# Attention operands made without copies, and one tile for the last queries of two heads, in a planned three-stage kernel

## The chip, the core and the metric

The kernel runs on one core of a Trainium2 chip. The metric is the device time of one execution in microseconds. The engines are named as in the profile: PE (TensorE, the matmuls; PEld its weight loads), DVE (VectorE), ACT (ScalarE), POOL (GpSimd) and SP (SyncE, which issues nearly all DMA transfers).

## What is computed

```
# _attn_ref: q, k, v are (4, 8, 576, 64); blocks of 64 positions, causal by block
scores = where(block_i >= block_j, q @ k.T / 8, -1e9)
attn   = exp(scores - max); attn /= sum + 1e-9;  x = attn @ v      # -> (2304, 512)
# _moe_ref: one expert layer for all tokens, d_ff = 1024
h = x @ w_in; solu = h * softmax(h); ln = (solu - mean) / sqrt(var + 1e-6) * g_ln
x = ln @ w_out
# _moe2_ref: cosine routing to the best of 8 experts, then that expert only
expert = argmax(xn @ en.T / tau);  out[token] = gate * (relu(x @ w1[expert]) @ w2[expert])
```

## The kernel before

Three stages follow each other: attention, a first expert layer over 18 tiles of 128 tokens, and a second one that works through tiles of gathered tokens, expert by expert. All matmuls work with numbers split in a high and a low part, so that one product is two or three matmuls.

**Attention** works on items. Items 0 to 3 ("low") each hold queries 0 to 255 of two heads of the first batch, so that the first tiles of tokens are complete early; then one item per head follows, without those queries for the first eight heads. `attn_load` brings q and k of an item into a buffer R (q in partitions 0 to 63, k in 64 to 127). `attn_prep` makes four operands H, L, S2, M2 from it, of which each matmul contracts 128 partitions: `it.ops = ((L, H), (S2, M2))`. A head's high and low parts have to lie in both halves of the partitions. For items 0 and 1 a second load with the halves exchanged (`qkl`, buffer RX) gives that; for the others H and L are made for 128 partitions at once, and four copies by DMA within SBUF put the halves in their places, two of them one after the other:

```
for o, on, x, xn in ((sb, Sa, hb[0:64], Ha), (mb, Ma, lb[64:128], Lb), (lb[64:128], Lb, sb[0:64], Sa),
                     (hb[0:64], Ha, hb[64:128], Hb)):
    op("SP", .45, lambda o=o, x=x: nc.sync.dma_start(o, x), r=["pa", xn], w=[on], size=W // 4)
```

There are three sets of operands, used in turn by items. `attn_score` then works through steps s0 to s4, tiles of 128 queries against 128, 256, 384, 512 and 576 keys; s4 has only 64 queries, 512 to 575. Per tile: two products on PE, a maximum (DVE), an exponential with its sum (ACT); per group of tiles (`it.norm`) a small addition to the sums (POOL), a reciprocal (DVE) and a scale of each tile (POOL or ACT, `either`). `attn_trans` (t0 to t4) transposes the probabilities on PE and evicts them into TH (ACT) and, as the rest, TL (DVE). `attn_av` (a0, a1) multiplies with V; the result goes to DRAM tensors `xT`, from which `b_load` brings tiles of tokens.

**The first expert layer** needs w_in and w_out converted from 64-bit floats by integer operations (`conv_ops`: three on DVE, then a cast on ACT and a subtract on POOL per piece) into the tile `win`; `b_up`, `b_down`, `b_route` and `b_choose` are its four parts per tile of tokens.

**The order** of these two stages is made by a planner (`order`): each operation has an engine, a duration and what it reads and writes; a list scheduler starts, on the engine that is free, the ready operation of the highest priority. The priority comes from a table of due times, `DUE`, by kind of work (A loads and operands, S scores, T transposes, V products with V, C weights, U, D, R the expert layer) and item, and from the transfers' time `land`. `either` operations go to the engine that is free first. What the planner puts in order stands so in each engine's queue, and an engine works through its queue in that order. The second expert layer is written out by hand (`c_all`).

## Time and profile before

| | before |
|---|---|
| median of 3 runs | 804.76 us (804.27 to 806.49) |
| profiled execution | 808.63 us, span 806.9 us |
| PE, DVE, ACT, POOL busy | 716.0, 472.4, 440.3, 313.4 us |
| mean granted clock of PE | 0.958 of full speed |
| moved by DMA | 101.02 MB, mean 125 GB/s |

PE's busy time counts from a matmul's start to its modelled end, and neighbours overlap in the pipeline; a matmul of 512 columns in a dense row starts 0.23 us behind the one ahead and is shown with 0.39 us. So a busy PE may still have gaps between its starts. Busy shares are means over stages with different limits; the rows below are therefore taken by stretches of the span.

### The profile page before, as it was taken

The numbers are of one execution on the slowest core, as the hardware profiler recorded it, in microseconds if no ns is written. First come the engines' busy times: TensorE is split into PE (matmuls) and PEld (weight loads), VectorE is DVE, ScalarE is ACT, GpSimd is POOL, SyncE is SP. The second block draws the span as 40 slices with busy tenths as digits, with TensorE's granted clock in tenths as the row PEclk, the third lists the DMA queues.
The fourth block names the chain that finished last, engine by engine and source line by source line (L and its number), as shares of the span: only waits on it lengthen the run. The fifth ranks groups of instructions, "written<-read, shape, count | busy, mean of one in ns | idle before, by whom it ended". The sixth has DMA issues, their size and how long they took to land. (4 is left out here: it accounts for less than half of the span.)

```text
span 806.9 us, 12838 instructions
## 1 busy us (share of the span) xinstructions
PE 716.0 (89%) x3832; PEld 575.0 (71%) x3832; DVE 472.4 (59%) x1055; ACT 440.3 (55%) x1019; POOL 313.4 (39%) x493
## 2 busy tenths in 40 slices
PE   1579887999989999989999999778999989989994
PEld 1467756877767788778887777567788867867883
DVE  5788879789948746868754766342222166266221
ACT  5688678888857656869553644211212255255211
POOL 4457456745727533665544544221111111111120
PEclk9989978999999999989999999889999999989998
DMA  8997655336371530363012600158111158167110
GB/s 228 240 255 221 184 165 154 100 103 176 101 191 58 153 91 25 102 154 79 28 53 64 222 27 28 40 192 312 34 46 50 40 180 296 42 207 265 40 42 23
DMA packets 59890, 101.02 MB, mean 125 GB/s; under 512 B 14288, under 2 KB 26224, under 8 KB 59792
## 3 DMA queue, kind: packets, MB, share of 16 engines
q1 hardware_dynamic: 55856, 89.44, 37.8%
q0 software_dynamic: 3936, 10.51, 3.7%
q8 instruction: 32, 0.52, 0.3%
q14 instruction: 66, 0.54, 0.3%
HBM read 65.42 MB, written 15.11 MB: 100 GB/s over the span
## 5 line engine op out<-in xcount | busy, mean ns | idle before, releaser
L555 PE MATMUL banks<-wexp,workr 128*128 128x512 f32 x320 | 135.8, 424 | 3.6 <-ACTq L1056 2.9
L556 PE MATMUL banks<-wexp,workr 128*128 128x512 f32 x320 | 129.9, 406 | 3.7 <-DVEq L1056 3.7
L557 PE MATMUL banks<-wexp,workr 128*128 128x512 f32 x320 | 129.3, 404 | 0.0
L555 PE MATMUL banks<-win,workr 128*128 128x512 f32 x288 | 123.5, 429 | 2.6 <-POOL workr L234 1.6
L543 DVE TENSOR_TENSOR workr<-banks,workr 128x512 fp32r<-128x512 f32 x61 | 42.2, 691 | 127.6 <-ACT workr L542 100.3
L557 PE MATMUL banks<-win,workr 128*128 128x512 f32 x288 | 115.6, 401 | 0.5 <-POOL workr L583 0.5
L556 PE MATMUL banks<-win,workr 128*128 128x512 f32 x288 | 115.5, 401 | 0.0
L436 PE MATMUL banks<-attr 128*128 128x256 f32 (+5 forms) x384 | 88.8, 357 | 29.4 <-POOL attr L388 12.4
L442 ACT ACTIVATE att<-banks,att 64x576 f32<-64x576 f32 (+4 forms) x160 | 89.7, 567 | 23.6 <-DVE att L439 20.2
L436 PEld LDWEIGHTS banks<-attr 128*128 128x128 f32 (+1 forms) x384 | 57.5, 191 | 44.7 <-POOL attr L388 12.4
L1016 ACT ACTIVATE work<-banks 128x512 f32<-128x512 f32 x40 | 23.9, 596 | 119.3 <-PE banks L557 119.2
L439 DVE TENSOR_REDUCE att<-banks 64x1 f32<-64x576 f32 (+4 forms) x160 | 80.3, 534 | 12.9 <-PE banks L436 12.1
L1044 POOL DMA_INDIRECT out<-work x20 | 20.1, 1004 | 161.2 <-DVE work L1043 141.8
L475 PE MATMUL banks<-work,att 128*128 128x128 f32 (+1 forms) x480 | 69.2, 279 | 13.6 <-POOL att L234 5.5
L484 DVE TENSOR_TENSOR attr<-banks,attr 128x128 fp32r<-128x128 f32 (+4 forms) x160 | 70.7, 483 | 17.9 <-ACT attr L481 17.0
L520 PE MATMUL banks<-attr 128*128 128x320 f32 (+9 forms) x504 | 71.0, 288 | 6.5 <-DVE att L450 2.2
L520 PEld LDWEIGHTS banks<-attr 128*128 128x128 f32 (+1 forms) x504 | 65.5, 162 | 14.1 <-ACT att L442 4.1
L556 PEld LDWEIGHTS banks<-wexp,workr 128*128 128x128 f32 x320 | 62.5, 195 | 17.1 <-DVEq L1056 5.2
L555 PEld LDWEIGHTS banks<-wexp,workr 128*128 128x128 f32 x320 | 62.3, 195 | 16.9 <-ACTq L1056 4.0
L557 PEld LDWEIGHTS banks<-wexp,workr 128*128 128x128 f32 x320 | 61.9, 194 | 15.3 <-DVE workr L543 0.5
L475 PEld LDWEIGHTS banks<-work,att 128*128 128x128 f32 (+1 forms) x480 | 51.3, 148 | 28.2 <-POOL att L234 8.5
L542 ACT ACTIVATE workr<-banks 128x512 fp32r<-128x512 f32 x61 | 36.4, 597 | 63.6 <-PE banks L1027 52.1
(210 smaller groups left out, 1293.6 us busy)
## 6 DMA issues: line engine op xcount, KB each, us to landing
raw<-in_w SPq DMA_DIRECT2D x28, 1024.0 KB, 7.8
attr<-attr SPq DMA_DIRECT2D x128, 144.0 KB, 3.6
att<-in_kq SPq DMA_DIRECT2D x32, 288.0 KB, 4.0
att<-in_v SPq DMA_DIRECT2D x16, 320.0 KB, 5.2
x2d<-work SPq DMA_DIRECT2D x19, 256.0 KB, 3.6
work<-xT SPq DMA_DIRECT2D x14, 256.0 KB, 7.2
work<-in_w_in SPq DMA_DIRECT2D x5, 512.0 KB
xT<-att SPq DMA_DIRECT2D x16, 160.0 KB, 4.0
```

What stands on the lines that cost most here:

```text
L436: nc.tensor.matmul(ps.ap[:P, a:b], st[:, q0:q0 + P], mv[:, k0 + a:k0 + b], start=y == 0, stop=y == 1, skip_group_check=True)
L439: op("DVE", .15 + .00104 * W, lambda j=j, W=W, P=P, ps=ps: nc.vector.reduce_max(nm[:P, j:j + 1], ps.ap[:P, 0:W], axis=X, negate=True), r=[ ...
L442: op("ACT", .45 + .00086 * W, lambda j=j, W=W, P=P, e=e, ps=ps: nc.scalar.activation(E[:P, e:e + W], ps.ap[:P, 0:W], AF.Exp, bias=nm[:P, j ...
L475: nc.tensor.transpose(ps.ap[:, o:o + Q], E[:Q, a:a + 128], c.ident[:Q, :Q])
L484: lambda src=src, dh=dh, dl=dl: nc.vector.tensor_tensor(dl(), src(), dh().bitcast(F32), op=ALU.subtract),
L520: nc.tensor.matmul(o, a, b, start=k == 0, stop=k == len(mm) - 1, skip_group_check=True)
L542: h = c.nc.scalar.activation(H, ps, AF.Copy)
L543: return h, c.nc.vector.tensor_tensor(L, ps, H.bitcast(F32), op=ALU.subtract)
L555: nc.tensor.matmul(o, ah, bh, start=first, stop=False)
L556: nc.tensor.matmul(o, ah, bl, start=False, stop=False)
L557: nc.tensor.matmul(o, al, bh, start=False, stop=last)
L1016: c.mark[ENG.Activation] = nc.scalar.activation(d["u"][:, w], o, AF.Relu).ins
```

## The change

Six items (`DIRECT = range(6)`: the four low ones and the first head pair) make all four operands with engine operations that read the half of R they need, whichever partitions it lies in, and write the half that is wanted; `qkl` and RX are gone. R has two names, Ra and Rb, for its halves. The last 64 queries of an even head and of the odd head behind it (its `mate`) become rows 0 to 63 and 64 to 127 of one tile: the odd head's matmul runs with 128 stationary columns (queries 448 to 575, of which the upper half counts), then the even head's overwrites rows 0 to 63. Maximum, exponential, norm, scale and five transposes are then done once per pair; the eviction is one per head. `s4` and `t4` exist for odd heads alone; the even head's `a1` stands behind them. `norm` has s3 and s4 apart. For low items two tiles of one head are evicted together. The planner's numbers change: an SP issue costs .58 in place of .45, a transfer lands after 2.0 in place of 2.5 us at 255 in place of 280 GB/s, two-input operations that may run on DVE or POOL are kept apart on both, three operations of `conv_ops` become `either`, and the table of due times is new throughout.

```
-NORMS = [7]
-PREPH = [15, 18]
+DIRECT = range(6)
-            self.norm = {"s2": [0, 1, 2], "s4": [3, 4]}
+            self.norm = {"s2": [0, 1, 2], "s3": [3], "s4": [4]}
+            if n % 2 == 0:
+                del self.steps["s4"], self.steps["t4"]
 def either(op, eng, fn, r, w, **durs):
-    op(eng, durs[eng], lambda: fn(eng), r=r, w=w, lock=eng == "POOL",
-       alt=(other, durs[other], other == "POOL", lambda: fn(other)))
+    lock = lambda e: e == "POOL" or e == "DVE" and other == "POOL" or e == "DVE" and eng == "POOL"
+    op(eng, durs[eng], lambda: fn(eng), r=r, w=w, lock=lock(eng), alt=(other, durs[other], lock(other), lambda: fn(other)))
 def conv_ops(c, k, n):
-    op("ACT", .63, lambda: nc.scalar.activation(WH, f, AF.Copy), r=[an], w=["wh%d" % k])
-    op("POOL", 1.1, lambda: nc.gpsimd.tensor_tensor(WL, f, WH.bitcast(F32), op=ALU.subtract), r=[an, "wh%d" % k], w=["wl%d" % k],
-       lock=True)
+    either(op, "ACT", lambda e: scaled(c, e, WH, f, 1.0), ACT=.63, POOL=.63, r=[an], w=["wh%d" % k])
+    either(op, "POOL", lambda e: I(e).tensor_tensor(WL, f, WH.bitcast(F32), op=ALU.subtract), POOL=1.1, DVE=.73,
+           r=[an, "wh%d" % k], w=["wl%d" % k])
 def items():
+    for a, b in zip(its[4::2], its[5::2]):
+        b.mate, b.eb4 = a, b.n // 2 % 2
 def attn_load(c, it):
-    if i < 2:
-
-        it.RX = c.E[i][:, 0:512]
-        c.op("SP", .45, lambda: nc.sync.dma_start(it.RX, c.qkl[it.n]), r=["pa"], w=[("E%d" % i, 0, 512)], size=256)
 def attn_prep(c, it):
-    if i < 2:
+    if i in DIRECT:
+        either(op, "POOL", lambda eng: scaled(c, eng, S2[a], it.R[a], 1.0 / 8.0), ACT=d, POOL=.27 + .00083 * W, r=["pa", ra], w=[Sa])
+        op("ACT", d, lambda: scaled(c, "ACT", H[a], it.R[b], 1.0), r=["pa", rb], w=[Ha])
+        either(op, "POOL", lambda eng: scaled(c, eng, H[b], it.R[b], 1.0), ACT=d, POOL=.27 + .00083 * W, r=["pa", rb], w=[Hb])
+        op("ACT", d, lambda: scaled(c, "ACT", L[b], it.R[a], 1.0 / 8.0), r=["pa", ra], w=[Lb])
+        op("DVE", .08 + .0012 * W, lambda: nc.vector.scalar_tensor_tensor(L[a], it.R[a], 1.0 / 8.0, sb[a], op0=ALU.mult, op1=ALU.subtract),
+           r=["pa", ra, Sa], w=[La], lock=True)
+        op("DVE", .1 + .0013 * W, lambda: nc.vector.tensor_tensor(M2[a], it.R[b], hb[b], op=ALU.subtract), r=["pa", rb, Hb],
            w=[Ma], lock=True)
 def attn_score(c, it, step):
+        heads = [(it, q0, 128)] if P == 128 else [(it, q0 - 64, 128), (it.mate, q0, 64)]
+        for (x, qa, m) in heads:
+            def product(qa=qa, k0=k0, W=W, x=x, m=m, ps=ps):
...
+            op("PE", SCORE[W], product, r=["pa"] + x.opn, w=[ps])
+        P = 128
 def attn_trans(c, it, step):
+        for x, h in ((it, head),) if not last else ((it.mate, 0), (it, 1)):
+            cols = [(x.addr(h, ch, 128 * i), x.addr(h, ch, 128 * i) + Q) for ch in chs]
+            ev.append((off + 64 * h * last, Q, i + 1, cols))
+    if it.low:
+        ev = [(a[0], 128, 3, a[3] + b[3]) for a, b in zip(ev[0::2], ev[1::2])]
-            nc.tensor.transpose(ps.ap[:, o:o + Q], E[:Q, a:a + 128], c.ident[:Q, :Q])
+            nc.tensor.transpose(ps.ap[:, o:o + 128], E[:, a:a + 128], c.ident)
 class Rates:
-    pool, turn, land, rate = .12, .07, 2.5, 280.
+    pool, turn, land, rate = .12, .07, 2., 255.
 def stages(c, dag):
+            if x == "a" and hasattr(it, "mate"):
+                key("V", it.i - 1)
+                attn_av(c, it.mate, "a1")
 DUE = dict(
-    Z=[586.3],
+    Z=[1309.7],
...
```

On SP, which issues the transfers, the program begins so before (`in_kql` and `in_kq` are loads of q and k, `in_qkl` the exchanged ones, `in_w_in` pieces of w_in, `attr<-attr` the copies within SBUF):

```order
L329 DMA att<-in_w_in 128x1024
L257 DMA work<-in_g 128x8
L355 DMA att<-in_kql 128x512
L360 DMA att<-in_qkl 128x512
L363 DMA att<-in_mask 64x576 x2
L355 DMA att<-in_kql 128x512
L360 DMA att<-in_qkl 128x512
L412 DMA att<-in_v 128x256 x2
```

and so now:

```order
L258 DMA work<-in_g 128x8
L360 DMA att<-in_kql 128x512
L364 DMA att<-in_mask 64x576 x2
L360 DMA att<-in_kql 128x512
L413 DMA att<-in_v 128x256 x2
L330 DMA att<-in_w_in 128x1024
L277 DMA work<-in_tau 128x1
```

The first piece of w_in has moved behind the loads of the first two items, and the two exchanged loads are gone. Up to the first load of a tile of `xT` there were 29 copies within SBUF, and there are 12.

On PE the first scores of a head's last queries stand so before (L436 are score matmuls, L520 products with V, L475 transposes; 64x512 and 64x64 are the 64 queries against 512 and 64 keys):

```order
L436 MATMUL banks<-attr 128x512 x2
L520 MATMUL banks<-attr 64x256 x3
L520 MATMUL banks<-attr 64x128 x3
L436 MATMUL banks<-attr 64x512
L436 MATMUL banks<-attr 64x64
L436 MATMUL banks<-attr 64x512
L436 MATMUL banks<-attr 64x64
```

and now (L441 and L543 are the same two lines):

```order
L441 MATMUL banks<-attr 128x512 x3
L441 MATMUL banks<-attr 128x64
L441 MATMUL banks<-attr 128x512
L441 MATMUL banks<-attr 128x64
L441 MATMUL banks<-attr 64x512
L441 MATMUL banks<-attr 64x64
L441 MATMUL banks<-attr 64x512
L441 MATMUL banks<-attr 64x64
```

The odd head's four matmuls, 128 rows wide, come first, and the even head's four follow at once; before, a head's four stood by themselves.

## Rows read from the trace of the kernel before

**Rows 1.** The page: its first line, and DMA share in 40 slices.
```profile
span 806.9 us, 12838 instructions
DMA  8997655336371530363012600158111158167110
```

**Rows 2.** By stretches: length, busy us (instructions) per engine, clock, DMA share, GB/s.
```profile
0.00:70.00 70.00, 37.31 (x191) 30.44 (x192) 51.18 (x121) 46.50 (x125) 33.99 (x67) 0.95 0.90 238
70.00:416.00 346.00, 323.28 (x1956) 261.73 (x1955) 260.56 (x584) 258.77 (x659) 191.14 (x308) 0.96 0.42 116
416.00:506.00 90.00, 88.83 (x467) 69.95 (x465) 54.64 (x146) 41.91 (x82) 42.18 (x71) 1.00 0.27 85
...
20.00:40.00 20.00, 10.38 (x46) 8.85 (x46) 15.39 (x37) 12.11 (x38) 9.12 (x14) 1.00 0.95 237
200.00:220.00 20.00, 19.49 (x138) 16.15 (x137) 18.29 (x46) 17.69 (x51) 15.26 (x26) 1.00 0.33 90
```

**Rows 3.** Transfers of 0:70: totals, then issues, KB each, median us to landing.
```profile
DMA packets 9343, 16.68 MB, mean 238 GB/s; under 512 B 1464, under 2 KB 3672, under 8 KB 9338
...
attr<-attr SPq DMA_DIRECT2D x25, 144.0 KB, 4.2
...
att<-in_qkl SPq DMA_DIRECT2D x2, 256.0 KB
```

**Rows 4.** Timeline of PE: start us, us, line, tiles, forms [idle before <-releaser].
```profile
12.39 0.47 PE L436 MATMUL banks<-attr 128*128 128x128 f32 x1 [12.39 <-POOL attr L388]
...
70.35 0.48 PE L555 MATMUL banks<-win,workr 128*128 128x512 f32 x1
...
414.10 1.73 PE L520 MATMUL banks<-attr 128*128 128x256 f32 x14
...
505.91 0.40 PE L557 MATMUL banks<-win,workr 128*128 128x512 f32 x1
510.72 1.11 PE L998 MATMUL banks<-work 128*128 128x128 f32 x4 [4.41 <-DMA work<-x2d,work]
```

**Rows 5.** Timelines of POOL and DVE in 0:40.
```profile
10.61 1.14 POOL L344 TENSOR_TENSOR win<-work,win 128x512 fp32r<-128x512 f32 x1
11.72 0.61 POOL L388 TENSOR_SCALAR attr<-att 64x512 fp32r<-64x512 f32 x1
...
24.52 2.13 POOL L344 TENSOR_TENSOR win<-work,win 128x512 fp32r<-128x512 f32 x2
...
12.80 0.67 DVE L394 TENSOR_TENSOR attr<-att,attr 64x512 fp32r<-64x512 f32 x1
...
24.60 2.60 DVE L394 TENSOR_TENSOR attr<-att,attr 64x512 fp32r<-64x512 f32 x1
```

**Rows 6.** Groups by form, whole span: busy us, mean ns, idle before and releaser.
```profile
L475 PEld LDWEIGHTS banks<-work,att 128*128 128x128 f32 x320 | 38.4, 150 | 20.8 <-POOL att L234 8.5 <-ACT att L232 4.9 <-issue 3.7
...
L439 DVE TENSOR_REDUCE att<-banks 64x1 f32<-64x576 f32 x32 | 23.6, 742 | 1.8 <-PE banks L436 1.2 <-ACT att L442 0.5
L442 ACT ACTIVATE att<-banks,att 64x576 f32<-64x576 f32 x32 | 23.4, 731 | 2.8 <-DVE att L439 2.4
...
L234 POOL TENSOR_SCALAR att<-att 64x576 f32<-64x576 f32 x16 | 13.4, 838 | 5.3 <-DVE att L450 5.2
...
L448 POOL TENSOR_SCALAR att<-att 128x1 f32<-128x1 f32 x8 | 3.3, 411 | 1.5 <-ACT att L442 1.0
...
L377 ACT ACTIVATE attr<-att 64x576 fp32r<-64x576 f32 x3 | 1.9, 674 | 0.1
...
L387 ACT ACTIVATE attr<-att 64x512 fp32r<-64x512 f32 x2 | 1.3, 629 | 4.8 <-DMA att<-in_kql 4.8
...
L450 DVE RECIPROCAL att<-att 128x1 f32<-128x1 f32 x8 | 1.2, 146 | 0.0
```

**Rows 7.** Waits in 70:416: who for whom, us in total, times, longest.
```profile
POOL att L448 <- ACT att L442: 25.9, 18, 5.7
...
PE banks L436 <- DMA attr<-attr: 3.7, 2, 2.3
```

More of the change, by code (lines that the diff above doesn't have):

```diff
@@ L458, in attn_trans @@
     op, nc = c.op, c.nc
-    E, en = c.E[it.eb], "E%d" % it.eb
-    ps = c.group(f"t{it.i}_{step}")
+    js = it.steps[step]
+    last = it.q[js[0]][3] == 64
+    eb = it.eb4 if last else it.eb
+    E, en = c.E[eb], "E%d" % eb
+    ps = c.group(f"t{it.i}_{step}", 2 if last else 1)
     off, ev, tr, reads = 0, [], [], []
-    for j in it.steps[step]:
+    for j in js:
         _, _, _, Q, e, head, i = it.q[j]
         down = it.addr(head, 1, 0) < it.addr(head, 0, 0)
-        chs = list(range(i + 1))[::-1] if down else list(range(i + 1))
-        tr += [(off + x * Q, Q, e + 128 * ch) for x, ch in enumerate(chs)]
+        chs = list(range(i + 1))[::-1] if down and not last else list(range(i + 1))
+        tr += [(off + x * 128, e + 128 * ch) for x, ch in enumerate(chs)]
@@ L467, in attn_trans @@
         reads.append((en, e, e + 128 * (i + 1)))
-        stride = abs(it.addr(head, 1, 0) - it.addr(head, 0, 0))
-        ev.append((off, Q, i + 1, it.addr(head, chs[0], 128 * i), stride,
-                   [(it.addr(head, ch, 128 * i), it.addr(head, ch, 128 * i) + Q) for ch in chs]))
-        off += (i + 1) * Q
-    def transposes():
-        for o, Q, a in tr:
-            nc.tensor.transpose(ps.ap[:, o:o + Q], E[:Q, a:a + 128], c.ident[:Q, :Q])
-    op("PE", .03 + (.09 if Q == 128 else .087) * len(tr), transposes, r=["pa"] + reads, w=[ps])
@@ new lines, in transposes, with src @@
+    def transposes():
+        for o, a in tr:
+            nc.tensor.transpose(ps.ap[:, o:o + 128], E[:, a:a + 128], c.ident)
+    op("PE", .03 + .09 * len(tr), transposes, r=["pa"] + reads, w=[ps])
+    for (off, Q, nch, cols) in ev:
+        rise = cols[0][0] <= cols[-1][0]
+        base, stride = min(a for a, _ in cols), abs(cols[1][0] - cols[0][0]) if nch > 1 else Q
+        def src(off=off, Q=Q, nch=nch, rise=rise):
+            v = ps.ap[:, off:off + (nch - 1) * 128 + Q]
+            if nch == 1:
+                return v.rearrange("p (c q) -> p c q", q=Q)
+            ap = [list(x) for x in v.ap]
+            return bass.AP(v.tensor, v.offset if rise else v.offset + (nch - 1) * 128,
+                           [ap[0], [128 if rise else -128, nch], [1, Q]])
@@ L1485, in moe_attention_kernel @@
 @with_exitstack
[L1486 removed]
+def moe_attention_kernel(ctx, tc, kq, kql, mask, v, w_in, w_out, g, emb, emb32, tau, w1, w2, out):
     nc = tc.nc
     c = Ctx()
[L1489 removed]
+    c.kq, c.kql, c.mask, c.v, c.g_d, c.emb_d, c.tau_d, c.w1_d, c.w2_d, c.out = kq, kql, mask, v, g, emb, tau, w1, w2, out
     c.emb32 = emb32
```

128 lines of the change are left out of this document (60 added, 68 removed).

## The prediction

> **What bounds the kernel now.** I read the page first, for the span and the line of the transfers [rows 1]. They are dense in the first four of the forty slices, some 80 us, and never again so for long in the first half. So I cut the span where the PE timeline shows the stages to change: its first matmul is at 12.39 us, the first matmul of the first expert layer (tile `win`) at 70.35, the last at 505.91; then PE waits 4.41 us for gathered rows, and the second expert layer runs to the end. The last attention matmuls start at 414.10 [rows 4]. So the view by stretches is asked for 0:70, 70:416 and 416:506, and for two denser pieces [rows 2].
>
> The reader is to see four regimes there. From 416 to 506 PE is busy 88.83 of 90 us: nothing but matmuls counts, and the change leaves those matmuls as they are. Behind 506 nothing is edited. In 70:416 PE is idle for 346 − 323.3 = 22.7 us by the profile; DVE and ACT are busy about 260 us each, three quarters. The weak stretch is 0:70: PE busy 37.3, so 32.7 us idle; DVE 51.2, ACT 46.5, and the DMA engines at a share of 0.90, moving 238 GB/s. That is the one place where a resource off PE is close to full, and PE has no filler there, since the first `win` matmul needs the queries 0 to 255 of eight heads and converted weights. The transfer view of the same stretch says what fills it: 16.68 MB, among them 25 copies of 144 KB within SBUF (and eight smaller), 4.2 us each from issue to landing, and two extra loads of `qkl` [rows 3]. What happens up to 70 us is therefore paid once, and everything behind it is shifted by it.
>
> **The change part by part.**
>
> *Copies and early loads.* Six items instead of two make their score operands directly. Over the program 16 of 136 copies within SBUF go, and both `qkl` loads. What counts is what stands in SP's order ahead of the first load of a tile of `xT`, with which the first expert layer starts: 29 copies become 12 (2,320 KB less), two `qkl` loads go (512 KB), one piece of `w_out` falls behind (512 KB), one store of `xT` comes in front (160 KB). That is 15.65 MB before and 12.39 MB after, 3.26 MB less; at the 238 GB/s of [rows 3] 13.7 us. The loads of the first item also move ahead of the first piece of `w_in`, so that the first matmul, which waited for a POOL operation at 11.72 us, itself behind a weight subtract [rows 5], comes earlier; that is a part of the 13.7 us and not added.
>
> In exchange the operands are made by engines. ACT gets 10 more operations of 64x512 at 0.629 us and 6 more of 64x576 at 0.674 us [rows 6], 10.3 us, nearly all in this stretch, against some 3 us that it loses there (the 128-row casts of four items, and eight evictions that become part of a longer one); 46.5 + 7 = 53.5 us. In its densest stretch ACT is busy 17.69 of 20 us, a share of 0.885 [rows 2]; at that it needs 53.5 / 0.885 = 60.5 us. DVE trades 128-row subtracts for pairs of 64-row ones and stays near 51 us; at its densest, 18.29 of 20, that is 56 us. The bytes would allow 70.4 − 13.7 = 56.7 us. The latest is ACT: the first `win` matmul at about 60.5 us, a gain of 10 us. The ends are 0 (the engines stay as loosely packed as now) and 14 us (the bytes alone); I take 10, since the densest rows show that the engines can be packed so.
>
> The Trainium skill, "DMA: Bandwidth & Descriptors", section "Anatomy of one DMA", has about 2.0 us fixed and the rest at 436 GB/s for a transfer. By that rate the 3.26 MB would be 7.5 us, an estimate from the page; the rows' 238 GB/s and 4.2 us for 144 KB (2.3 us by the page) say that the engines are shared here, and the measured rate decides.
>
> *The last 64 queries of two heads as one tile.* Per pair of heads one maximum, one exponential, one scale and five transposes go; the score matmuls are as many and as wide as before (64 rows become 128 for half of them, and PE's time goes by columns). DVE: 16 × 0.742 = 11.9 us less. ACT: 16 × 0.731 = 11.7 us less. The scale, on POOL or ACT: 16 × 0.838 = 13.4 us less. New: the norm of items is cut finer, so there are 16 more small additions on POOL (0.411 us, 6.6 us) and 16 more reciprocals on DVE (0.146 us, 2.3 us) [rows 6]. Seven subtracts of weights go from POOL (1.14 us at 10.61 [rows 5]) to DVE (0.67 us, the nearest two-input row at 12.80 [rows 5]): 8.0 us less there, 4.7 us more here. DVE ends 4.9 us lower, ACT 1.4 with the 10.3 from above, POOL and the scales 14.8: 21 us of the 710 that the three are busy in 70:416, 3%. A gain here can at most be PE's idle 22.7 us, and all of DVE's 11.9 us would be the reach of this edit; 0 is the other end. I take 4 us, a third, because three engines at 55 to 75% are not full: what PE waits for are chains, and shorter links help some of them. PE itself: 160 transposes of 64 queries become 80 of 128. If each cost its weight load, 0.150 us [rows 6], 80 fewer are 12 us; if the columns that move count, nothing, for 160 × 64 = 80 × 128. I take 1 us, near the lower end, since PE is busy for longer than its weight loads in every stretch [rows 2].
>
> *What it ties together.* The last tile of a pair needs the operands of both heads, so those of the even head are held until then, and both heads' second product with V stands behind that tile. The wait of such a chain is in the list: POOL's small addition waited for ACT's exponential 25.9 us in 18 waits, 1.44 us each [rows 7]. POOL is in order, so what stands behind it there, scales and the operand casts of the next head, waits too. If every one of 16 pairs pays it on PE, 23 us; if the finer norm only splits a wait that is there now, 0. I take 2 us, since PE has expert matmuls to fill in from the first batch on (the order below has them between the pieces), and PE's own wait for copies within SBUF, which follow those casts, was only 3.7 us here [rows 7].
>
> *Due times and the planner's rates* set the order and no duration. Nothing in the trace prices them; they could at most remove the 22.7 us of idle, and as much the other way. I take 0.
>
> *Two-input subtracts on DVE beside POOL.* At 12.80 us such a subtract took 0.67 us, at 24.60 the same took 2.60 while POOL ran two subtracts from 24.52 on [rows 5]. The Trainium skill, "SBUF — State Buffer", section "Who interferes with whom", says that a DVE instruction with two SBUF inputs and a POOL instruction that reads SBUF exclude each other for a whole instruction; the trace agrees, with 1.93 us. The change puts 11 such subtracts more on DVE (four for operands, seven for weights), and takes seven off POOL. I count 0 for it and keep it as a rival.
>
> Sum: −10 − 4 − 1 + 2 = −13 us. The profiled execution took 808.63 us (its span is 806.9, 1.7 us lie around it), so 795.6 for such an execution. The median of the timed runs, 804.76, is 3.9 us below it, which gives 791.8, forecast as 792.
>
> **The rivals.**
>
> *The start stays engine-bound.* For it: in the new order ACT has more of the attention's work ahead of the first tile's softmax, and neither it nor DVE is over 0.92 busy even where densest. Against it: the DMA share of 0.90 to 0.95 in 0:70 and 20:40 [rows 2], higher than any engine's. Then the 10 us are gone: −4 − 1 + 2 = −3, 802.
>
> *DVE and POOL collide.* 11 subtracts at 1.93 us more are 21 us of DVE; with POOL busy 34 of 70 us [rows 2] half of them, 10 us, and in the first 110 us, where DVE is needed. −13 + 10 = −3, 802 as well.
>
> *The pairs stall (slower).* Place: the norm of the last tile, between ACT's exponential and the scale on POOL, 16 times. Price 1.44 us each, 23 us; without my 2 us the sum is −15, so 804.8 − 15 + 23 = 813. It decides from the point where more than two thirds of these waits reach PE. Against it: the filler matmuls. For it: nothing that comes before the first batch's end has a filler, and the even head's V products now come in one burst with the odd one's.
>
> *All of it pays.* Start by the bytes, −14, and DVE's 11.9 us in full: −14 − 12 − 1 = −27, 778.
>
> **How the numbers follow.** Forecast 0.53, with its own range 784 to 799 (start 5 to 14 us, the middle 0 to 8). Start engine-bound 0.13, collision 0.07, pairs stall 0.15, all of it pays 0.12. A measurement of this kernel tells about 0.3% from no change, 2.4 us: under 802.4 is faster, over 807.2 slower. The forecast but for 0.02, the last rival, and half of the two that give 802 are faster: 0.51 + 0.12 + 0.10 = 0.73; same 0.12; slower 0.15. The range 778 to 810 leaves out half of the last rival and most of the slow one, less than 2 in 10.
>
> **What would show it.** Right: the first `win` matmul at 57 to 64 us with the DMA share still 0.85 or more up to it; the first matmul at 8 to 10 us; ACT over 0.8 busy up to there; the time from the last attention matmul to the last `win` matmul unchanged at about 90 us; PE idle after the start below 22 us up to there. Wrong: the first `win` matmul at 68 us or later (the bytes were not the bound); DVE subtracts of over 1.5 us in numbers (collision); POOL's waits for the exponential above 40 us in sum, and PE waits for scales or for copies within SBUF beside them (the pairs). A time over 807 can only come from the middle stretch or from a start that is not shorter.

## The result and the profile after

The median fell from 806.32 us (803.79 to 810.18) to 795.17 us (790.55 to 799.86), eight runs of each: a ratio of 0.9873, 95% interval 0.9839 to 0.9907. The forecast was 792 us with 778 to 810 around it, a gain of 13 us; the runs show 11.2. Ratios, here and below, leave out executions in a slower state, those more than 1.5% above the fastest of the same kernel, so a ratio need not be the quotient of the medians beside it.

The profiled execution took 791.86 us, span 790.2, against 808.63 and 806.9. First the page of the changed kernel, its first line and the share of the transfers in 40 slices, which answer to [rows 1]:

```profile
span 790.2 us, 12576 instructions
DMA  6578665557523217342211700158111166167010
```

The first four slices, 8997 before, are 6578 now: the start is no longer dense with transfers. Then the stretches, with the limits where the stages of this kernel lie (to its first `win` matmul, and from there to the end of its last); after the stretch's limits and length come busy us and instructions of PE, PEld, DVE, ACT and POOL, the granted clock, the DMA share and GB/s:

```profile
0.00:65.20 65.20, 37.63 (x201) 31.29 (x201) 51.77 (x116) 52.39 (x127) 33.70 (x71) 0.97 0.71 211
65.20:491.60 426.40, 397.39 (x2332) 325.48 (x2330) 305.84 (x714) 285.88 (x710) 229.62 (x380) 0.98 0.42 113
```

The same two of the kernel before, asked for with its own limits:

```profile
0.00:70.35 70.35, 37.66 (x197) 30.79 (x197) 51.53 (x122) 46.83 (x126) 33.99 (x67) 0.95 0.90 239
70.35:506.30 435.95, 412.06 (x2418) 331.33 (x2415) 315.05 (x730) 300.39 (x738) 233.31 (x378) 0.97 0.39 110
```

Two things are to be seen. In the start the DMA share fell from 0.90 to 0.71, while ACT went from 46.83 of 70.35 us to 52.39 of 65.2, from two thirds to four fifths; the stage is 5.15 us shorter. In the middle, 9.6 us shorter, PE is busy 14.7 us less and idle 29.0 us where it was idle 23.9: its busy time is shorter and it waits more.

The points of the PE timeline that answer to [rows 4]: first matmul, first and last `win` matmul, the wait for gathered rows.

```profile
7.59 0.47 PE L441 MATMUL banks<-attr 128*128 128x128 f32 x1 [7.59 <-ACT attr L233]
...
65.17 0.48 PE L578 MATMUL banks<-win,workr 128*128 128x512 f32 x1
...
491.16 0.40 PE L580 MATMUL banks<-win,workr 128*128 128x512 f32 x1
500.06 1.12 PE L1021 MATMUL banks<-work 128*128 128x128 f32 x4 [8.50 <-DMA work<-x2d,work]
```

The first line says most about the start. The first matmul comes at 7.59 us in place of 12.39, 4.8 us earlier, and from it to the first `win` matmul it is 57.6 us now and was 58.0. So nearly all of the 5.2 us is there before any matmul has run, with the loads of the first item ahead of the first piece of w_in; behind that point the bytes that went and the work that came leave the length as it was, to within the 2 us by which two executions differ (below). No run isolates that earlier beginning.

The last line is a loss that the forecast has no term for: PE waits 8.50 us there, 4.41 before. From the end of the last `win` matmul to the first of the second expert layer it is 10.3 us now and 6.2 before. Behind that point, where nothing was edited, this execution took 288.3 us and the one before 294.4. The kernels below took 286.2 to 289.3 there, those with the code of before among them (288.9 and 289.3), so those 6.1 us are a property of the one profiled execution of before, and no gain of the change. The account by stages is −5.1 − 9.6 + 4.1 = −10.6 us, near the 11.2 of the medians. Each of its terms comes from one execution of each kernel, though, and the next section shows how far two executions of one order lie apart.

### The profile page after: what moved, and what is told of

Its sections match the earlier page's. It is cut to its first block, busy times and chain, and to the rows that moved or that the text cites. A ratio compares the mean times of both kernels' runs of the same rounds, so it can differ in the third digit from the quotient of the medians.

```text
span 790.2 us, 12576 instructions
## 1 busy us (share of the span) xinstructions
PE 697.7 (88%) x3752; PEld 566.4 (72%) x3752; DVE 465.0 (59%) x1045; ACT 431.7 (55%) x992; POOL 309.3 (39%) x498
## 5 line engine op out<-in xcount | busy, mean ns | idle before, releaser
L578 PE MATMUL banks<-win,workr 128*128 128x512 f32 x288 | 121.1, 421 | 2.5 <-DVE work L626 1.1
L579 PE MATMUL banks<-win,workr 128*128 128x512 f32 x288 | 114.2, 396 | 0.0
L580 PE MATMUL banks<-win,workr 128*128 128x512 f32 x288 | 114.1, 396 | 0.0
L441 PE MATMUL banks<-attr 128*128 128x512 f32 (+6 forms) x384 | 86.5, 353 | 21.9 <-ACT attr L233 7.6
L1039 ACT ACTIVATE work<-banks 128x512 f32<-128x512 f32 x40 | 23.9, 597 | 117.8 <-PE banks L580 117.6
L448 ACT ACTIVATE att<-banks,att 128x128 f32<-128x128 f32 (+4 forms) x144 | 78.5, 550 | 13.2 <-DVE att L445 11.6
L441 PEld LDWEIGHTS banks<-attr 128*128 128x128 f32 (+1 forms) x384 | 58.3, 195 | 34.6 <-ACT attr L233 12.0
L445 DVE TENSOR_REDUCE att<-banks 128x1 f32<-128x128 f32 (+4 forms) x144 | 70.4, 512 | 18.9 <-PE banks L441 18.3
L507 DVE TENSOR_TENSOR attr<-banks,attr 128x320 fp32r<-128x320 f32 (+4 forms) x152 | 70.6, 499 | 17.2 <-ACT attr L504 16.3
L489 PE MATMUL banks<-work,att 128*128 128x128 f32 x400 | 65.3, 296 | 15.7 <-ACT att L233 13.1
L543 PE MATMUL banks<-attr 128*128 128x320 f32 (+9 forms) x504 | 69.5, 284 | 9.9 <-DVE attr L507 8.3
L543 PEld LDWEIGHTS banks<-attr 128*128 128x128 f32 (+1 forms) x504 | 64.0, 158 | 18.3 <-ACT att L448 7.5
L579 PEld LDWEIGHTS banks<-wexp,workr 128*128 128x128 f32 x320 | 61.7, 193 | 16.9 <-DVEq L1079 5.2
L578 PEld LDWEIGHTS banks<-wexp,workr 128*128 128x128 f32 x320 | 61.4, 192 | 17.0 <-ACTq L1079 4.3
L580 PEld LDWEIGHTS banks<-wexp,workr 128*128 128x128 f32 x320 | 61.2, 191 | 16.1 <-DVE workr L566 1.6
L504 ACT ACTIVATE attr<-banks 128x320 fp32r<-128x320 f32 (+4 forms) x152 | 61.0, 453 | 12.5 <-PE banks L489 11.7
```

What stands on the lines that cost most here:

```text
L441: nc.tensor.matmul(ps.ap[:m, a:b], st[:, qa:qa + m], mv[:, k0 + a:k0 + b], start=y == 0, stop=y == 1, skip_group_check=True)
L445: op("DVE", .15 + .00104 * W, lambda j=j, W=W, P=P, ps=ps: nc.vector.reduce_max(nm[:P, j:j + 1], ps.ap[:P, 0:W], axis=X, negate=True), r=[ ...
L448: op("ACT", .45 + .00086 * W, lambda j=j, W=W, P=P, e=e, ps=ps, E=E: nc.scalar.activation(E[:P, e:e + W], ps.ap[:P, 0:W], AF.Exp, bias=nm[ ...
L489: nc.tensor.transpose(ps.ap[:, o:o + 128], E[:, a:a + 128], c.ident)
L504: op("ACT", .18 + .00083 * nch * Q, lambda src=src, dh=dh: nc.scalar.activation(dh(), src(), AF.Copy), r=["pa", ps], w=[("TH", a, b) for a ...
L507: lambda src=src, dh=dh, dl=dl: nc.vector.tensor_tensor(dl(), src(), dh().bitcast(F32), op=ALU.subtract),
```

## The experiments

Twelve kernels ran, in three lots; each lot has its own runs of the kernel before (medians of all of them 801.71, 804.0 and 802.91 us), and each ratio is to those. "Over the changed kernel" is the ratio less 0.9873, times that median; with both intervals it is uncertain by about 4 us, by 5 to 6 where a ratio's own interval is wider. The changed kernel itself did not run again in these lots, so every such difference goes by way of the kernel before. By plain medians against the changed kernel's 795.17, the four kernels in its own order come out as twice +10.3, casts2 +4.2, bytes2 +0.3 and tail −4.7 us. The stages are those of the one profile that each kernel has: first `win` matmul, from there to the end of the last one ("middle"), and from that to the second expert layer ("gap").

| kernel | ratio to before (95%) | over the changed kernel, us | first `win` | middle | gap |
|---|---|---|---|---|---|
| before | 1 | 11.2 | 70.35 | 436.0 | 6.2 |
| changed | 0.9873 (0.9839 to 0.9907) | 0 | 65.2 | 426.4 | 10.3 |
| old_due | 1.0132 (1.0079 to 1.0186) | 20.8 | 76.0 | 443.0 | 5.1 |
| new_due | 1.0421 (1.0363 to 1.0480) | 43.9 | 75.9 | 461.4 | 9.7 |
| copies_back | 1.0109 (1.0050 to 1.0167) | 18.9 | 70.3 | 439.8 | 10.1 |
| no_tile | 1.0357 (1.0294 to 1.0421) | 38.8 | 65.9 | 460.0 | 11.4 |
| jitter1 | 1.0096 (1.0058 to 1.0133) | 17.9 | 72.6 | 437.5 | 10.1 |
| jitter2 | 1.0237 (1.0185 to 1.0289) | 29.2 | 79.7 | 444.0 | 9.9 |
| jitter_before | 1.0193 (1.0138 to 1.0248) | 25.7 | 79.5 | 442.2 | 4.8 |
| bytes | 1.0250 (1.0205 to 1.0295) | 30.3 | 73.8 | 454.3 | 10.3 |
| twice | 1.0022 (0.9991 to 1.0052) | 12.0 | 66.6 | 440.1 | 10.0 |
| casts2 | 0.9994 (0.9956 to 1.0033) | 9.7 | 70.6 | 431.2 | 9.5 |
| bytes2 | 0.9922 (0.9886 to 0.9958) | 3.9 | 67.7 | 430.2 | 9.5 |
| tail | 0.9836 (0.9790 to 0.9881) | −3.0 | 67.3 | 427.8 | 4.0 |

How far do two executions of one order differ? tail (like the others described below), whose four moved due times change no engine's order before 455 us, is a second profile of the changed kernel up to there. Its first `win` matmul comes 2.1 us later, 67.3 for 65.2. Up to 55 us the two agree within 0.3 us; then the same 12 score matmuls take 3.80 us, at a granted clock of 0.56, where they took 2.24 at 1.00. The changed kernel's stretch, and then that of tail:

```profile
56.60:58.90 2.30, 2.24 (x12) 1.69 (x12) 1.24 (x4) 1.55 (x4) 1.56 (x1) 1.00 1.04 389
```

```profile
57.20:61.10 3.90, 3.80 (x12) 2.80 (x12) 1.35 (x4) 1.32 (x2) 0.98 (x1) 0.56 0.99 354
```

A difference of 2 us in a stage of this table is therefore no finding by itself. The middle has such spells too. Of the `win` matmuls that follow another at once, 16 start about 0.43 us behind it in the profile of the kernel before, 1 in that of the changed kernel, where most stand 0.23 apart: some 3 us of the 9.6 are the clock of those two executions, in these matmuls alone. One such spell of the kernel before, at a granted clock of 0.51:

```profile
233.40:236.90 3.50, 3.50 (x10) 2.72 (x10) 0.82 (x1) 0.94 (x2) 1.15 (x2) 0.51 0.93 228
```

Among the kernels in the changed order, tail and casts2 show 1 of them, twice 13 and bytes2 14, so it isn't the order that decides.

### The table and the edits apart

old_due is the changed code with the table of before; new_due is the code of before with the changed table and the planner's new rates.

```
 old_due:      DUE = dict(Z=[586.3], X=[2200.3], C=[89.4, 3221.8, ...     # in place of Z=[1309.7], ...
 new_due:      DUE = dict(Z=[1309.7], X=[2512.8], C=[715.7, 4029.6, ...   # in place of Z=[586.3], ...
```

Expected of old_due: 

> The changed kernel with the old table of due times (the planner's rates stay new). Theory: the edits to the operands and to the last tile carry most of the gain, the table does not: 796 to 800 us, first matmul of the first expert layer (tile win) at 64 to 68 us. Rival, the table carries it: 804 us or more, the old time, with PE idle spread over the middle stretch.

Expected of new_due: 

> The kernel before with the new table of due times and the new rates, and nothing else of the change. Theory, the edits carry the gain: 803 to 812 us, first win matmul at 68 us or later, since the bytes ahead of it stay. Rival, the table carries it: 794 to 799 us.

Measured: each half alone makes the kernel slower than before, by 1.3% and 4.2%, and both together make it 1.3% faster. By its time old_due falls to its rival, and its first `win` matmul comes at 76.0 us, not at 64 to 68; new_due is slower than both of its theories allow, its first `win` matmul as late as foreseen (75.9). An account by addition (so much the edits, so much the table) is not to be had from these two.

### One edit undone

```
 copies_back:  -DIRECT = range(6)       +DIRECT = range(2)
 no_tile:      -            if n % 2 == 0:
               -                del self.steps["s4"], self.steps["t4"]
               -        heads = [(it, q0, 128)] if P == 128 else [(it, q0 - 64, 128), (it.mate, q0, 64)]
               +        heads = [(it, q0, P)]
```

Expected of copies_back: 

> The changed kernel in which items 2 to 5 have their copies within SBUF again (items 0 and 1 stay direct). Theory, the start is paid by those copies: first win matmul back at 68 to 72 us and 798 to 802 us. Rival, ACT bounds the start whatever the copies do: first win at 63 to 66 us and 794 to 796 us, as ACT has 8 of its added casts less.

Expected of no_tile: 

> The changed kernel in which each head keeps its last 64 queries as a tile of its own (16 more maxima, exponentials and scales, 160 transposes of 64 queries). Theory, as predicted: start unchanged (first win at 64 to 67 us), the middle stretch 4 us longer: 797 to 801 us. Rival, the shared tile ties pairs together and costs as much as it saves: 793 to 796 us. A second rival, it carries the whole middle: 803 us or more.

Measured: the start did what it should. With the copies the first `win` matmul stands at 70.3 us, where the kernel before has it; with separate tiles it stays at 65.9. In the start of copies_back, 0:70, PE waits for the copies to land (us in total, times, longest):

```profile
PE banks L441 <- DMA attr<-attr: 7.0, 2, 3.9
```

The changed kernel has no such wait there, and the kernel before has 0.9 us of it. But the two kernels lost 13 and 34 us in the middle, where the copies of items 2 to 5 don't lie at all, and where the tile saves no engine more than 12 to 15 us. Both kernels carry a table that was made for other operations, and these two runs can't tell that misfit from the part that was undone.

### How much the order alone is worth

So the next kernels left all code as it is and moved every due time by a random amount within 50 units, a small step beside the hundreds by which the change moved them: twice for the changed kernel, once for the one before.

```
 jitter1, jitter2:  DUE = {k: [v + uniform(-50, 50) for v in V] for k, V in DUE.items()}   # changed kernel, two draws
 jitter_before:     the same on the kernel before, with its own table
```

Expected of jitter1: 

> The changed kernel with every due time of the planner's table moved by a random amount within 50 units (its entries go from -2,900 to 27,900, and the change moved them by hundreds); every instruction stays, its place in the queues moves a little. Theory A, the gain hangs on the very table that goes with the edits, since a due time that is off by little lets a wait into a queue: a ratio of 0.995 or above, with the loss spread over the middle stretch. Theory B, small shifts of the order cost nothing, and the 10 to 42 us of the earlier runs come from a table that was far from the edits: 0.984 to 0.991.

Expected of jitter2: 

> The changed kernel with every due time moved by another random amount within 50 units. Theory A, any move of this size costs about as much (the first such kernel stood at 1.0096): 1.000 to 1.020. Theory B, the first one happened on a bad order, and the next stands near the table as it is: 0.984 to 0.994.

Expected of jitter_before: 

> The kernel before with every due time of its own table moved by a random amount within 50 units, as was done with the changed kernel (809.88 us, ratio 1.0096, against 0.9873 unmoved). Theory A, each table fits its own kernel by a hair and both lose alike: a ratio of 1.012 or above here, so that the edits are worth about as much under two moved tables as under two that fit. Theory B, only the new table is that sharp, since its edits tie more operations together: 1.005 or below, and the edits without a fitted order are worth nothing.

Measured: 18 and 29 us lost by the changed kernel, 15.5 us by the one before (0.0193 of 802.91). Theory A holds for all three (jitter2 lies even above its range): in three draws of three a random step away from the table costs more than the whole change brings. The loss isn't in the middle alone, as was expected of jitter1: of 7.4 + 11.1, 14.5 + 17.6 and 9.1 + 6.2 us the first term is the start's. The stretches of jitter2, by its own limits, show how:

```profile
0.00:79.70 79.70, 40.88 (x225) 33.72 (x225) 62.48 (x138) 56.70 (x136) 34.42 (x71) 0.85 0.66 192
79.70:523.70 444.00, 405.11 (x2307) 328.15 (x2305) 299.33 (x710) 276.58 (x686) 225.03 (x375) 0.97 0.37 105
```

PE is idle 38.8 us of the start (27.6 unmoved) and 38.9 of the middle (29.0). No engine is busy for a larger share there than in the unmoved kernel, and the DMA share is lower too. That leaves waits in queues that stand in a worse order, and more work ahead of the first `win` matmul (225 matmuls in place of 201). The middle's busy time is 7.7 us higher too, at a granted clock of 0.97. Over the whole span the runs of the three moved kernels show a mean granted clock of 0.951 to 0.957, those of the changed one 0.964; whether that is a cause of the loss or comes of it, no run separates.

Read beside this, old_due (1.0132) and copies_back (1.0109) lie where two random draws lie (1.0096 and 1.0237) and say nothing of the part they undo. Under moved tables the edits' own worth doesn't show at all, 1.0096 and 1.0237 with them and 1.0193 without.

### The start: bytes or ACT

From here on kernels whose order stays as it is count. A first attempt, bytes, did not keep to that: it put 11 transfers of 288 KB, planned like others, behind the first loads.

```
 bytes:   for j in range(2 if i < 5 else 1 if i == 5 else 0):
              c.op("SP", .58, lambda scr=scr, j=j: nc.sync.dma_start(scr, c.kq[2 * i + j]), w=["scr%d_%d" % (i, j)])
```

Expected of bytes: 

> The changed kernel with 11 transfers of 288 KB more (from one place in DRAM to another, read by nobody), two behind the loads of each of the first five items and one behind the sixth's: 3.2 MB, about what the change took off the transfers of the start. Theory A, the start is bound by bytes (the prediction's step): the first matmul of the first expert layer moves back by 10 to 14 us, from 65 to 75 us or later, and the whole by as much, a ratio of 0.999 or above. Theory B, the start is bound by ACT, which makes the operands: the DMA share before that point goes from 0.71 to above 0.8, the first such matmul comes at 64 to 68 us, and the ratio is 0.986 to 0.992.

Measured: nothing held these transfers, so all were issued between 0.8 and 11.2 us, ahead of the loads that the first items need; the first matmul came at 13.6 us instead of 7.6, and the order behind it changed. Its 30 us can't be told from the price of that, and the question stays open. Two kernels answered it. bytes2 hangs the same transfers on the loads of items 2 to 7 so that no engine's order moves; casts2 runs ACT's two fixed casts of each directly made item twice, 12 operations.

```
 bytes2:  c.op("SP", .58, lambda: [nc.sync.dma_start(it.R, ...)] + [nc.sync.dma_start(s, c.kq[2 * i + j - 4]) for j, s in enumerate(scr)], ...
 casts2:  op("ACT", d, lambda: [scaled(c, "ACT", H[a], it.R[b], 1.0) for _ in range(2)], r=["pa", rb], w=[Ha])
          op("ACT", d, lambda: [scaled(c, "ACT", L[b], it.R[a], 1.0 / 8.0) for _ in range(2)], r=["pa", ra], w=[Lb])
```

Expected of bytes2: 

> The changed kernel in its own order, with the same 11 transfers of 288 KB that nobody reads, now issued two at a time right behind the loads of items 2 to 6 and one behind that of item 7 (8 to 35 us), so that nothing moves in any engine's order and the first item's loads are not held up. Theory A, the start is bound by bytes: the first matmul of the first expert layer goes from 65 to 73 us or later, at a DMA share above 0.85 in 0:65, and the ratio to the kernel before is 0.998 or above. Theory B, the transfers have room and the start is bound by the engines' work: that matmul comes at 64 to 68 us with the share above 0.85, and the ratio is 0.986 to 0.992. A move of the start without a higher share would say that the transfers are late one by one (their latency), not full in sum.

Expected of casts2: 

> The changed kernel in its own order, with the two casts of each directly made item that are fixed to ACT executed twice (12 operations more of 0.63 to 0.67 us, 7.8 us of ACT, all before the first matmul of the first expert layer). Theory A, ACT is the bound of the start: that matmul moves from 65 to 71 us or later and the whole by as much, a ratio of 0.995 or above. Theory B, ACT has 14 us of idle time there (busy 52 of 65) and takes the casts up in it: at most 67 us, and 0.986 to 0.990.

Measured, the start of bytes2 and then that of casts2, each by its own limits:

```profile
0.00:67.70 67.70, 37.90 (x200) 31.36 (x201) 51.26 (x116) 52.11 (x127) 31.63 (x70) 0.82 0.82 251
```

```profile
0.00:70.60 70.60, 36.55 (x200) 30.17 (x201) 51.69 (x115) 60.27 (x139) 32.78 (x71) 0.98 0.67 197
```

By the first `win` matmul alone 3.2 MB more cost 2.5 us and ACT's 7.9 us more (60.27 − 52.39) cost 5.4; but tail, with nothing added, has that matmul 2.1 us late. A cleaner mark is a matmul some 14 us ahead of it, behind all the added transfers and casts. It is the 145th in each of these kernels, and here are its lines in the changed kernel, tail, twice (described below; hardly anything is added to it so far), bytes2 and casts2:

```profile
51.11 0.33 PE L543 MATMUL banks<-attr 128*64 128x320 f32 x1 [0.66 <-ACT attr L504]
...
50.99 0.33 PE L543 MATMUL banks<-attr 128*64 128x320 f32 x1 [0.65 <-ACT attr L504]
...
51.45 0.33 PE L544 MATMUL banks<-attr 128*64 128x320 f32 x1 [0.64 <-issue]
...
52.88 0.33 PE L545 MATMUL banks<-attr 128*64 128x320 f32 x1 [0.66 <-ACT attr L506]
...
56.14 0.33 PE L543 MATMUL banks<-attr 128*64 128x320 f32 x1 [0.66 <-ACT attr L504]
```

Three executions without additions agree within 0.5 us there; bytes2 is 1.8 us behind the changed kernel and casts2 5.0. So up to there ACT's work costs about two thirds of each microsecond added. The transfers cost 1.8 us of the 13.3 that the forecast's 238 GB/s would give, about an eighth. Theory B holds for bytes2 in kind, its DMA share of 0.82 and ratio of 0.9922 just outside what was named; casts2 is theory A's, 0.4 us short of its 71. For the whole, casts2 is 9.7 us over the changed kernel by the ratio and 4.2 by plain medians, bytes2 3.9 and 0.3: casts2 is slower, bytes2 can't be told from nothing.

One thing bytes2 doesn't price. Nobody waits for its transfers, whereas the copies that went stood in the chain that makes the operands; the 7.0 us of copies_back are such waits, under a table that does not fit it. What the copies cost by being waited for, in a fitted order, stays open.

What ACT's lateness does is in the waits of PE and PEld for its casts (L233 writes operands into `attr` and scaled probabilities into `att`), here in 0:66 of the changed kernel, and then of casts2: who for whom, us in total, times, longest.

```profile
PEld banks L441 <- ACT attr L233: 12.0, 2, 7.6
...
PEld banks L489 <- ACT att L233: 7.5, 6, 3.3
...
PE banks L489 <- ACT att L233: 6.1, 3, 3.1
```

```profile
PEld banks L441 <- ACT attr L233: 16.8, 3, 9.1
```

The score matmuls' wait for operands grows from 12.0 to 16.8 us. One place of it in the changed kernel, ACT's timeline and then PE's (start us, us, line):

```profile
19.89 4.68 ACT L233 ACTIVATE attr<-att 64x576 fp32r<-64x576 f32 x7
24.59 0.80 ACT L233 ACTIVATE att<-att 128x128 f32<-128x128 f32 x2
```

```profile
22.28 0.28 PE L299 MATMUL banks<-work 32*128 32x32 f32 x1 [2.98 <-DVE work L296]
25.05 1.09 PE L489 MATMUL banks<-work,att 128*128 128x128 f32 x3 [2.48 <-ACT att L233]
```

Seven operand casts stand in a row in ACT's queue, 4.68 us, ahead of the scale of two tiles for which PE's transposes wait.

### What the shared tile's engine time is worth

twice runs the maximum and the exponential of each shared 128x576 tile two times, in the order as it is.

```
 twice:   again = range(1 + (it.q[j][3] == 64))
          ... [nc.vector.reduce_max(nm[:P, j:j + 1], ps.ap[:P, 0:W], axis=X, negate=True) for _ in again]
          ... [nc.scalar.activation(E[:P, e:e + W], ps.ap[:P, 0:W], AF.Exp, ..., accum_out=SM[:P, j:j + 1]) for _ in again]
```

Expected of twice: 

> The changed kernel in its own order, with the maximum and the exponential of each shared tile of last queries executed twice (same inputs, same outputs), so that DVE and ACT get back the 16 x 0.74 us and 16 x (0.73 + 0.19) us that the shared tile saves, and nothing moves in any queue. Theory A, the saved time of DVE and ACT reaches the end in part (a third of DVE's 11.9 us, the prediction's term): 3 to 6 us over the changed kernel, a ratio to the kernel before of 0.991 to 0.995. Theory B, these engines have the room, and what the shared tile brings is the order that it allows: within 2 us of the changed kernel, 0.985 to 0.990. Theory C, DVE's and ACT's time is the bound of the middle: the whole of it, 12 us or more, 1.002 and above.

Measured: 12.0 us by the ratio, 10.3 by plain medians and 13.7 in the middle of the profile, so theory C, at its lower edge. The groups of the changed kernel and of twice, by form (busy us, mean ns):

```profile
L445 DVE TENSOR_REDUCE att<-banks 128x1 f32<-128x576 f32 x16 | 12.0, 750 | 5.0 <-PE banks L441 4.9
L448 ACT ACTIVATE att<-banks,att 128x576 f32<-128x576 f32 x16 | 11.9, 741 | 3.5 <-DVE att L445 3.5
```

```profile
L446 DVE TENSOR_REDUCE att<-banks 128x1 f32<-128x576 f32 x32 | 24.1, 754 | 7.2 <-PE banks L441 6.6
L449 ACT ACTIVATE att<-banks,att 128x576 f32<-128x576 f32 x32 | 23.7, 742 | 12.1 <-DVE att L446 8.3 <-DVE att L457 2.0 <-PE banks L655 1.3
```

DVE gets 12 us more and ACT 15 (12 of exponentials and 16 readings of their sums, 0.2 us each), and the end moves by 10 to 14, though DVE is busy 72% of the changed kernel's middle and ACT 67%. The two stages of twice show the form of the loss:

```profile
0.00:66.60 66.60, 37.20 (x201) 30.72 (x201) 53.31 (x118) 54.30 (x131) 34.49 (x71) 0.85 0.71 211
66.60:506.70 440.10, 405.00 (x2332) 328.72 (x2330) 314.26 (x727) 296.93 (x738) 228.91 (x379) 0.98 0.40 109
```

The start is hardly longer. In the middle PE, with the same 2332 instructions, is idle 35.1 us (29.0) and busy 7.6 us longer. Some 2.5 us of it are the clock: the 13 `win` matmuls named above, at 0.43 us in place of 0.23. Four of them lie in 87.5:89.7, where the granted clock is 0.51. The doubled operations stand one behind the other in a pair's chain, so that a longer chain (about 1.7 us for each of 16 pairs) and fuller engines come together here; which of the two makes the 12 us wasn't separated.

### The gap before the second expert layer

tail moves four due times, the choice of the expert for tiles 12 to 15, so that their counts and scatters stand some 20 `win` matmuls earlier on the queues.

```
-    R=[..., 463.5, 1479.5, 1141.3, 4177.9, 3338.1, 4008.5, 4014.],)
+    R=[..., 463.5, -500., -500., -500., -500., 4008.5, 4014.],)
```

Expected of tail: 

> The changed kernel with four due times moved (R of tiles 12 to 15, the choice of the expert, set to -500), so that the counts and scatters of these tiles go out about 20 win matmuls earlier, as in the kernel before. Theory A, the wait of 10.3 us between the last win matmul and the second expert layer is the chain of scatters on POOL, each waiting for the one ahead of it to land, which starts too late: the wait shrinks to 5 to 7 us and the ratio to 0.980 to 0.984. Theory B, the wait ends with the last tile's own scatter whatever the others do: the wait stays at 9 us or more, 0.986 to 0.990. Theory C, other due times make another order and the middle loses more than the wait gives: 0.990 or above with a wait below 8 us.

Measured: the gap is 4.0 us, theory A and below its range; the time is 3.0 us lower, which its uncertainty of 4 to 5 can't tell from nothing. The last scatters and the first gather on POOL, of the kernel before, the changed kernel and tail (start us, us, [idle before <-releaser]), with the scatter ahead of it for the changed kernel:

```profile
499.79 1.02 POOL L753 DMA_INDIRECT meta<-work  x1 [2.08 <-DVE ef L810]
...
506.60 1.09 POOL L987 DMA_INDIRECT work<-x2d,work  x1 [5.18 <-DVE work L744]
```

```profile
484.90 1.01 POOL L776 DMA_INDIRECT meta<-work  x1 [2.40 <-PE banks L654]
...
489.96 0.98 POOL L776 DMA_INDIRECT meta<-work  x1 [3.85 <-DMA meta<-work]
...
496.42 1.09 POOL L1010 DMA_INDIRECT work<-x2d,work  x1 [4.87 <-SPq L841]
```

```profile
487.06 1.02 POOL L776 DMA_INDIRECT meta<-work  x1 [2.66 <-DVE work L772]
...
494.04 1.09 POOL L1010 DMA_INDIRECT work<-x2d,work  x1 [3.83 <-DMA work<-meta]
```

From the last scatter to the gather it is 6.5 to 7.0 us in all three. What differs is where that scatter stands against the end of the `win` matmuls: 6.5 us ahead of it before, 1.6 in the changed kernel (its scatter had to wait 3.85 us for the landing of the one ahead), 8.0 in tail.

## Why the prediction was right, point by point

**The sum was right by luck.** The gain was forecast within 2 us, out of terms that were not right: −10 for the start was −5.1; −4, −1 and +2 for the middle were −9.6; the gap's +4.1 had no term. The errors cancelled. The time was 3.2 us off, 1.6 of them because the median of the kernel before is 806.32 us in eight runs and was 804.76 in the three that the forecast started from. Of the five signs named for being right only one came, ACT over 0.8 busy; none of the three for being wrong did.

**The start: the bound was misnamed.** Two marks of the forecast failed: the first `win` matmul at 57 to 64 us (65.17, short of the 68 that would have called it wrong), and a DMA share of 0.85 or more (0.71). The first matmul, at 8 to 10 us by the forecast, came at 7.59, and ACT over 0.8 busy held by a hair, 52.39 of 65.2. That first matmul, counted as a part of the bytes' gain, is itself as large as the stage's whole gain, 4.8 of 5.2 us. The ACT work was well forecast, 53.5 us against 52.4. The step that failed is the next one: that ACT could be packed at the 0.885 of its densest 20 us through the whole stage, since "the densest rows show that the engines can be packed so". At the 0.80 that it reached the forecast work gives 66.6 us, close to what came. The transfers were dense before, as read, but the price of the bytes removed was too high: as many bytes put back where nobody waits for them cost 1.8 us at 51 us and at most 2.5 at the first `win` matmul. The rival "the start stays engine-bound" described the mechanism better; its price, nothing gained at all, was too hard.

The Trainium skill, "DMA: Bandwidth & Descriptors", section "Anatomy of one DMA", gives 2.0 us and 436 GB/s for one transfer that GpSimd issues; these transfers are issued by SP, so the forecast's 7.5 us from that rate was an estimate by the nearest figure. The at most 2.5 us of bytes2 are below it as well. Neither rate is the price here, where the transfers lie beside the engines' work.

**The shared tile: four was probably too low.** "Three engines at 55 to 75% are not full" was the reason to take a third of DVE's 11.9 us. In the run twice, which gives DVE's and ACT's maxima and exponentials their time back, the end moves by 10 to 14 us. That isn't quite what the tile saved: twice puts the second operation into the same pair's chain, where two separate tiles would have two chains. But it shows that a mean share over 346 us doesn't price such work. The forecast's balance of the middle also charged ACT the 10.3 us of casts that lie in the start; without them the three engines were to lose 31 us there and not 21. By the stretches shown above they lost 27.4 (DVE 9.2, ACT 14.5, POOL 3.7).

**The transposes: one was five or six, in PE's busy time.** By form up to 520 us, the kernel before:

```profile
L475 PE MATMUL banks<-work,att 128*128 128x128 f32 x320 | 53.7, 298 | 13.0 <-POOL att L234 5.5 <-DVE attr L484 2.6 <-ACT att L442 2.5
L475 PE MATMUL banks<-work,att 64*128 64x64 f32 x160 | 17.2, 240 | 0.6 <-DVE att L242 0.4 <-DVE att L450 0.2
```

and the changed one:

```profile
L489 PE MATMUL banks<-work,att 128*128 128x128 f32 x400 | 65.3, 296 | 15.7 <-ACT att L233 13.1 <-POOL att L235 1.1 <-DVE attr L507 1.0
```

160 of 64 columns are busy 17.2 us, 0.107 each, and the 80 of 128 that replace them 65.3 − 53.7 = 11.6, 0.145 each: neither by columns nor by weight loads, but half-way, 5.6 us. No run shows how much of it reaches the end.

**The terms don't add up, and that stays open.** 10 to 14 us for the tile's operations and 5.6 for the transposes are more than the 9.6 that the middle gained, and PE's idle time rose there from 23.9 to 29.0 us, where the forecast had it fall below 22. The new order may cost some microseconds; but the clock's part in the 9.6, some 3 us, the 2 us between executions and the uncertainty of 4 are as large as what is missing. No run isolates it.

**The pairs did not stall.** POOL's wait for the exponential in the middle, 25.9 us in 18 waits before [rows 7], is:

```profile
POOL att L454 <- ACT att L448: 22.8, 19, 3.4
```

The rival at 813 us falls: the sum is no larger than before, and the longest of these waits is 3.4 us where it was 5.7.

**DVE and POOL collided no more than before.** The subtracts of two inputs that the change puts on DVE, those for the operands (0.67 and 2.60 us before [rows 5]; two more, of 64x576, take 0.75 us in the mean) and seven for weights, over the whole span:

```profile
L394 DVE TENSOR_TENSOR attr<-att,attr 64x512 fp32r<-64x512 f32 x4 | 3.2, 831 | 1.0 <-ACT attr L233 0.9
...
L346 DVE TENSOR_TENSOR win<-work,win 128x512 fp32r<-128x512 f32 x7 | 5.3, 764 | 0.4 <-ACT win L233 0.4
```

The dearest of them took 1.2 us, so the rival's 10 us fall. That the planner keeps such operations apart doesn't show as plainly: of the 30 subtracts of 128x576 three took 1.5 to 2.1 us beside a POOL operation, and before none of the 34 of that line took over 1.3. The dearest of the three, merged with the one ahead of it, and POOL's operation there:

```profile
187.84 2.85 DVE L400 SCALAR_TENSOR_TENSOR attr<-att,attr 128x576 fp32r<-128x576 f32 x2
...
187.95 2.13 POOL L419 TENSOR_TENSOR attr<-att,attr 128x640 fp32r<-128x640 f32 x1
```

**Due times at zero: right in the sum, wrong in the reason.** The bound was PE's 22.7 us of idle either way. Random steps cost up to 29 us, the wrong table 34 over the kernel before. Taking 0 amounts to assuming that the new table fits the new code about as well as the old one fitted the old code. No row of the trace gave that; the moved kernels, 15.5 us worse on one side and 18 and 29 on the other, agree with it and don't prove it. "Unchanged at about 90 us" for the time from the last attention matmul to the last `win` matmul failed too. The last attention matmuls of the changed kernel end at 385.3 us:

```profile
382.73 2.56 PE L543 MATMUL banks<-attr 128*128 128x320 f32 x20
```

From there it is 106 us, since the new table finishes attention earlier and leaves more `win` matmuls behind it, 357 for 312. The gap is part of that order: the choices of the last tiles moved towards the end.

## What to carry to other kernels

Where a table fitted to the code sets the order, undoing a part with the table left in place measures the misfit: here 19 to 44 us, for parts of a change that is worth 11 in all. Price a part with the order unmoved instead, by running its operations twice or hanging extra transfers on loads that are there; and take a control in which only the order moves before believing any difference of that size. Where one profile stands for a kernel, find a second one of the same order before reading a stage to 2 us. A full transfer system beside a busy engine is no proof of which one bounds a stage: what counts is how far the stage moves per microsecond added to each.

## What the runs showed of the hardware that was not expected

The DMA share doesn't go with the bytes. Before, 239 GB/s took a share of 0.90 in the start, with 25 copies within SBUF among the transfers; bytes2 moves 251 GB/s there at 0.82, with fewer such copies and 11 transfers from DRAM to DRAM (288 KB each, 5.0 us median to landing). So a share of 0.90 was not a limit in GB/s for such a mix.

The granted clock of a stage says little on its time, that of a dense group much. Up to 51 us twice shows 0.83 and the changed kernel 1.00, and twice is only 0.3 us behind there; PE is idle for 23 of those 51 us. But the 12 score matmuls that tail ran at 0.56 took 1.6 us longer, and 29 products with V in bytes2, at 0.67 in 53.7:58.8, 5.08 us for 3.55. That is 1.6 of tail's 2.1 us at the first `win` matmul, in a stage with nothing changed.
